# A spectral filter and gated unit: the filter's second copy made by VectorE and ScalarE, earlier x loads, a new timetable

## The chip, the cores and the metric

The kernel runs on one core of a Trainium2 chip. The core has a matrix engine (TensorE, PE in the profile), two vector engines (VectorE, DVE, and ScalarE, ACT), GpSimd (POOL) and SyncE (SP); the last two issue most of the DMAs here. The metric is device time in microseconds (us) of the whole kernel, the median over runs.

## What is computed

Each of 8 batches of x (3200 x 256) is filtered in the frequency domain along its 3200 rows, then goes through a gated linear unit with a causal convolution of 5 taps:

```python
X = np.fft.rfft(x, axis=1)
y = np.fft.irfft(X * (filt_r + 1j * filt_i)[None], n=3200, axis=1)
for k in range(5):
    gate_pre += conv_w[k] * yp[:, k:k + S, :]     # yp: y with 4 rows of zeros ahead
gate = 1.0 / (1.0 + np.exp(-gate_pre))
out = (gate * (y @ w_val)) @ w_out
```

## The kernel before

The transform over 3200 = 100 x 32 rows is done by matrix products, batch by batch. A batch passes these stages, whose short names are those of the tasks in the code:

- lx: GpSimd issues 8 DMAs that bring x as bf16 tiles xt (`load_x`, L201). s1: products with the first table (L468). so: eviction from PSUM to the tile so. t: VectorE transposes it in blocks into tt (L487).
- s2: products with the second table w_t (L497), in 7 groups u of two frequency slices (the last of one). xs: eviction. z: VectorE multiplies xs with the filter f_t (L513). ia: products with the inverse tables a_t and b_t (L528). ue: eviction into the tile u.
- The way back: batch 0 (the only one in TURN) is turned by VectorE, tasks k, from u into vt (`back`, L569). All other batches write u to a DRAM scratch (wr, L551) and read it back in another order (lv, L561), both issued by SP.
- ib: last inverse products (L579). ye: ScalarE evicts into yt (L588). ha: a small memset on GpSimd.
- For 7 blocks c of 512 rows: cv, the convolution on PE (L618, for batches 6 and 7 L632); ga, the sigmoid (L642); vl, the product with w_val (L652); gv, VectorE's product of both (L667); op, the product with w_out (L675); oe, eviction; st, the store issued by SP (L690).

Evictions so, xs, ue and oe may go to either vector engine; one helper, `copy`, does them (L459 on ScalarE, L461 on VectorE).

The filter tile f_t is 128 partitions x 2 (real, imaginary, index w) x 2 x 13 slices x 256, in bf16. GpSimd loads it in two cuts (FCUT: slices 0 to 5 and 6 to 12), each with w = 0 and 1, into partitions 0 to 31 (t = 0) and 64 to 95 (t = 1), three DMAs each, 24 in all (L261, L264, L267). Partitions 32 to 63 and 96 to 127 hold the same values once more. In `sp_setup` SP issues eight DMAs for that, from f_t to f_t (L294), each waiting for its three loads.

Behind the filter, `gate_loads` (task hold) lets GpSimd copy one value out of the last part of f_t (L449). Tasks lx of batch 1 on, and the loads of w_val and w_out (task wts, `load_w`), come behind it on GpSimd. pd is a memset of the unused part of batch 0's u (L544). cid, cia and cim build the last inverse table ci_t; here cid depends on the last transpose of batch 0.

The order of all instructions is fixed when the program is built. Class `Plan` holds tasks with an engine (or two) and a cost for each, dependencies, tiles taken and given back, and a rank. Its `run` plays them through in assumed time: whenever an engine is free, the ready task of least rank goes there. `stay` is added to the rank when PE would change between kinds of work, `lean` when a task that could go to ScalarE would go to VectorE. Each engine then executes its own instructions strictly in the order that came out; costs only shape that order. Transfers not in the plan (x of batch 0, the filter) are given by assumed landing times. The rank is a formula: for each stage a number from LAG (and FIRST for batch 0), 8 for each batch, and a STEP for each task of the stage.

Of the kernel before, what the change touches and what calls it, by code (L numbers as in the profile page):

```python
# [9 lines left out]
BF16 = mybir.dt.bfloat16  # L10
# [9 lines left out]
NM = 13  # L20
NV = 4 * NS
TURN = (0,)

LAG = dict(lx=-461, s1=-523, so=-124, t=307.5, pd=-178, s2=25, xs=106.5, z=302, ia=221,
           ue=176.5, k=-315, ib=312, ye=-498, cv=280, ga=-531.5, vl=-166.5, gv=-478, op=322.5,
           oe=-241.5)
FIRST = dict(lx=-94, s1=139, so=28.5, t=553.5, pd=153, s2=134, xs=-578.5, z=-363, ia=13, ue=-57,
             k=231.5, ib=193.5, ye=245.5, cv=72, ga=-202.5, vl=160, gv=-113, op=346.5, oe=277)
CONV = 1.2
SMALL = (6, 7)  # L30
STEP = dict(lx=0.95, s1=2.5, so=2.05, t=1.9, pd=0.75, s2=1.9, xs=0.25, z=1.15, ia=0.85, ue=2.25,
            k=0.1, ib=0.9, ye=1.65, cv=2.5, ga=2.2, vl=1.2, gv=0.95, op=1.35, oe=0.55)
STAY, LEAN = 32, 139
# [9 lines left out]
class Plan:  # L43
# [5 lines left out]
    def __init__(self, room, slots, stay=1.0, lean=0.0):  # L49
        self.tasks, self.room, self.stay = {}, dict(room), stay  # L50
        self.lean, self.slots = lean, list(range(slots))

    def add(self, name, engines, rank, deps, emit, take=(), give=(), land=0.0, mode=None,
            ps=0, free=()):
# [86 lines left out]
def kernel(  # L141
# [142 lines left out]
    def sp_setup():  # L284
# [162 lines left out]
    def gate_loads():  # L447
        hold = g1.tile([128, 1], BF16, name="hold")
        nc.gpsimd.tensor_copy(hold[...], f_t[:, 1, 1, NM - 1, 0:1])  # L449
# [245 lines left out]
    plan = Plan(dict(xt=NXT, so=1, t=1, xs=3, z=3, u=1, e=2, v=1, y=2, g=NGB, gv=NGB, o=NOB), 4,  # L695
# [6 lines left out]
    def dma(name, us, rank, dep, give=(), land=2.3, mode=0):  # L702
        add(name, {"DQ": us}, rank, dep, None, land=land, mode=mode)
        add(name + "+", {"none": 0.0}, rank, [name], None, give=give)

    for b in range(B):
        turned = b in TURN
        t0 = NCH * b

        def at(stage, n=0, b=b, t0=t0):  # L710
            return t0 + LAG[stage] + (FIRST.get(stage, 0) if b == 0 else 0) + STEP.get(stage, 1) * n

        for j in range(NCH):
            if b:
                add(f"lx{b},{j}", {"POOL": 0.6}, at("lx", j), ["hold"],
                    lambda e, b=b, j=j: load_x(b, j), take=("xt",), land=1.5)
                add(f"dx{b},{j}", {"DQ": 1.22}, at("lx", j), [f"lx{b},{j}"], None, land=2.0, mode=1)
            dep = [f"dx{b},{j}"] if b else [f"x0{j}", "cfa"]
            dep = dep + ([f"s1{b},{j - 1}"] if j else [])
            add(f"s1{b},{j}", {"PE": 0.45}, at("s1", j), dep, lambda e, b=b, j=j: s1(b, j),  # L720
                ps=1, take=("so",) if j == 0 else (), give=("xt",), mode=0)
            add(f"so{b},{j}", two(0.93, 1.14), at("so", j), [f"s1{b},{j}"],
                lambda e, b=b, j=j: so(b, j, e), free=[(f"s1{b},{j}", 0)])
        for q in range(4):
            add(f"t{b},{q}", {"DVE": 1.17}, at("t"), [f"so{b},{j}" for j in range(NCH)]
# [3 lines left out]
        add(f"pd{b}", {"POOL": 1.2} if turned else {"none": 0.0}, at("pd"),  # L729
            ["pool"] + ([f"pd{b - 1}"] if b else []),  # L730
            lambda e, b=b: pad(b), take=("u",) if turned else ("u", "e"))
        for u, (m0, nm) in enumerate(UCH):
            half = 0 if m0 + nm <= FCUT[0][1] else 1
            add(f"s2{b},{u}", {"PE": 0.11 * nm}, at("s2", u), ["wa"]
# [3 lines left out]
            add(f"xs{b},{u}", two(0.13 + 0.4 * nm, 0.04 + 0.55 * nm), at("xs", u),  # L738
                [f"s2{b},{u}"], lambda e, b=b, u=u: xs(b, u, e), free=[(f"s2{b},{u}", 0)])
            add(f"z{b},{u}", {"DVE": 0.06 + 0.55 * nm}, at("z", u), [f"xs{b},{u}", f"fl{half}"],  # L740
                lambda e, b=b, u=u: zed(b, u), give=("xs",))
            add(f"ia{b},{u}", {"PE": 0.22 * nm}, at("ia", u),
                [f"z{b},{u}", f"te{u // 2},1", f"pd{b}"],
                lambda e, b=b, u=u: inva(b, u), ps=1, give=("z",), mode=1)
            add(f"ue{b},{u}", two(0.13 + 0.4 * nm, 0.04 + 0.55 * nm), at("ue", u),
                [f"ia{b},{u}"], lambda e, b=b, u=u: ue(b, u, e), free=[(f"ia{b},{u}", 0)])
            if not turned:
                add(f"wr{b},{u}", {"SP": 0.45}, at("ue", u), [f"ue{b},{u}"],
                    lambda e, b=b, u=u: wr(b, u), land=1.0)
                dma(f"wq{b},{u}", 0.44 * nm, at("ue", u), [f"wr{b},{u}"])  # L750
        if turned:
            for q in range(4):
                add(f"k{b},{q}", {"DVE": 1.87}, at("k"), [f"ue{b},{u}" for u in range(len(UCH))]
# [3 lines left out]
        else:  # L757
            add(f"wd{b}", {"none": 0.0}, at("ue"), [f"wq{b},{u}+" for u in range(len(UCH))],
                None, take=("v",), give=("u",))
            for j in range(NCH):  # L760
                add(f"lv{b},{j}", {"SP": 0.8}, at("ib", j) - 2, [f"wd{b}"],
                    lambda e, b=b, j=j: lv(b, j), land=1.0)
                dma(f"lq{b},{j}", 0.68, at("ib", j), [f"lv{b},{j}"])
        for j in range(NCH):
            add(f"ib{b},{j}", {"PE": 0.37}, at("ib", j),
# [4 lines left out]
            add(f"ye{b},{j}", {"ACT": 0.79}, at("ye", j), [f"ib{b},{j}"],  # L770
                lambda e, b=b, j=j: ye(b, j), free=[(f"ib{b},{j}", 0)])
        add(f"ha{b}", {"POOL": 0.2}, at("ib"), [f"ye{b},0"], lambda e, b=b: halo(b))
        for c in range(NB):
# [3 lines left out]
            if c == p:  # L777
                add(f"cv{b},{c}", {"PE": CONV if tiny else 1.08 * f}, at("cv", c),
# [4 lines left out]
            add(f"ga{b},{c}", {"ACT": 0.77 * f + 0.16}, at("ga", c), [f"cv{b},{p}"],  # L783
# [82 lines left out]
```

## Time and profile before

| | us |
|---|---|
| median of 3 runs | 303.32 (301.4 to 303.38) |
| profiled execution | 303.88 |
| its span | 302.1 |
| PE busy | 261.7 (87%) |
| VectorE busy | 255.6 (85%) |
| ScalarE busy | 252.6 (84%) |
| GpSimd busy | 59.4 (20%) |

The mean granted TensorE clock is 0.969. In 40 equal slices of the span (7.55 us each), with the busy share in tenths:

```profile
PE   2831679889998799999989999999999999999992
DVE  7788788989999879999999999999998975466471
ACT  3964779999899788998899989999998978877863
PEclk9999956999999799999999999999999999999998
DMA  6999499999799979799998998748644994885656
```

A row reads from left to right in time; 9 is 90% or more. PEclk is the clock granted to PE in tenths of full speed. The engines work side by side, so a share of busy time doesn't tell by itself what sets the end.

### The profile page before, as it was taken

The page shows a single profiled execution, that of the slowest core. Times are in us where ns is not written, and L with a number is a line of the kernel's source. Part 1 is how long each engine was busy: PE and PEld are TensorE (multiplying, and loading weights), DVE is VectorE, ACT ScalarE, POOL GpSimd, SP SyncE. Part 2 cuts the span into 40 slices and gives each one's busy share as a digit, 9 for nine tenths or more (in the row PEclk, how much of TensorE's full clock was granted, in tenths as well). Part 3 has the DMA queues.
Part 4 walks back from the last instruction along what each step waited for, and adds up shares of the span by engine and source line. Part 5 has one row for each costly group of instructions (what it writes and reads, how often), then busy time and mean ns, then how long its engine had stood idle before and what let it go on. Part 6 is the DMA issues. An engine that isn't in the chain of part 4 may idle for free.

```text
span 302.1 us, 9397 instructions
## 1 busy us (share of the span) xinstructions
PE 261.7 (87%) x3924; PEld 158.1 (52%) x3924; DVE 255.6 (85%) x284; ACT 252.6 (84%) x301; POOL 59.4 (20%) x123
## 2 busy tenths in 40 slices
PE   2831679889998799999989999999999999999992
PEld 0121426345556435673567456745667667767661
DVE  7788788989999879999999999999998975466471
ACT  3964779999899788998899989999998978877863
POOL 8665457630140041004100400000000000000000
PEclk9999956999999799999999999999999999999998
DMA  6999499999799979799998998748644994885656
GB/s 91 189 163 166 89 175 134 151 189 237 197 252 261 369 187 225 216 330 294 236 278 283 241 249 248 248 177 257 215 160 183 315 326 156 297 289 203 242 203 239
DMA packets 53514, 67.70 MB, mean 224 GB/s; under 512 B 7840, under 2 KB 34336, under 8 KB 53472
## 3 DMA queue, kind: packets, MB, share of 16 engines
q1 hardware_dynamic: 41264, 51.79, 51.5%
q0 software_dynamic: 12208, 15.31, 31.8%
q8 instruction: 31, 0.51, 0.7%
q14 instruction: 11, 0.09, 0.1%
HBM read 42.54 MB, written 38.14 MB: 267 GB/s over the span
## 4 chain that ended last, share of the span: by engine, by line
PE 46%; ACT 18%; DVE 13%; DMA 12%; issue 5%; POOL 4%; ACTq 0%; DVEq 0%; POOLq 0%; SPq 0%
PE ps L675 12%; PE ps L652 10%; PE ps L618 10%; DMA xt<-in_x_dram 5%; ACT yt L588 5%; PE ps L579 4%; DVE gv L667 4%; DVE xs L461 4%; PE ps L528 3%; ACT gt L642 3%; DVE z L513 3%; ACT u L459 3%; PE ps L632 3%; POOL xt L201 2%; DMA f_t<-in_filt_r_dram 2%
## 5 line engine op out<-in xcount | busy, mean ns | idle before, releaser
L667 DVE TENSOR_TENSOR gv<-ps,gt 128x1024 bf16<-128x1024 f32 (+1 forms) x56 | 61.4, 1103 | 19.3 <-PE ps L652 14.7
L513 DVE TENSOR_TENSOR z<-xs,f_t 128x2048 bf16<-128x2048 bf16 (+1 forms) x56 | 62.3, 1140 | 1.9 <-DMA f_t<-f_t 1.4
L642 ACT ACTIVATE gt<-ps 128x1024 bf16<-128x1024 f32 (+1 forms) x56 | 50.9, 939 | 9.2 <-PE ps L618 5.5
L459 ACT ACTIVATE so<-ps 128x1024 bf16<-128x1024 f32 x51 | 49.7, 1031 | 8.2 <-PE ps L468 7.1
L588 ACT ACTIVATE yt<-ps 128x800 bf16<-128x800 f32 x64 | 51.2, 854 | 4.8 <-PE ps L579 4.7
L201 POOL DMA_DIRECT2D xt<-in_x_dram x64 | 35.4, 557 | 96.7 <-PE ps L468 66.2
L468 PE MATMUL ps<-xt,cf_t 100*128 100x512 bf16 x128 | 45.2, 443 | 9.8 <-DMA xt<-in_x_dram 6.7
L652 PE MATMUL ps<-yt,wv_t 128*128 128x512 bf16 (+1 forms) x224 | 52.5, 356 | 0.6 <-ACT xs L459 0.3
L675 PE MATMUL ps<-wo_t,gv 128*128 128x256 bf16 x400 | 51.2, 273 | 1.3 <-ACT yt L588 0.5
L618 PE MATMUL ps<-yt,dg_t 64*64 64x512 bf16 (+1 forms) x880 | 49.3, 357 | 1.3 <-ACT yt L588 1.1
L459 ACT ACTIVATE u<-ps 128x1024 bf16<-128x1024 f32 (+1 forms) x42 | 40.9, 989 | 9.7 <-PE ps L528 9.5
L459 ACT ACTIVATE o<-ps 128x1024 f32<-128x1024 f32 (+1 forms) x41 | 38.0, 938 | 7.1 <-PE ps L675 5.7
L675 PEld LDWEIGHTS <-gv 128*128 128x128 bf16 x400 | 37.2, 98 | 10.6 <-issue 2.9
L487 DVE STREAM_TRANSPOSE tt<-so 128x1024 f32<-128x1024 f32 x32 | 38.3, 1223 | 2.1 <-ACT so L459 2.1
L528 PE MATMUL ps<-z,a_t 64*64 64x256 bf16 x416 | 28.0, 288 | 11.5 <-DVE z L513 8.8
L579 PE MATMUL ps<-ci_t,vt 104*128 104x100 f16 (+1 forms) x512 | 33.5, 212 | 1.7 <-ACT u L459 0.6
L618 PEld LDWEIGHTS <-dg_t 64*64 64x64 bf16 x880 | 24.5, 108 | 18.0 <-issue 5.1
L579 PEld LDWEIGHTS <-vt 104*128 104x128 bf16 (+1 forms) x512 | 28.7, 100 | 10.0 <-issue 5.1
L461 DVE CAST xs<-ps 128x1024 bf16<-128x1024 f32 (+1 forms) x30 | 33.2, 1127 | 0.0
L497 PE MATMUL ps<-tt,w_t 64*64 64x256 bf16 x416 | 23.0, 292 | 8.2 <-DVE tt L487 5.6
L652 PEld LDWEIGHTS <-wv_t 128*128 128x128 bf16 x224 | 19.3, 97 | 17.7 <-issue 3.4
L459 ACT ACTIVATE xs<-ps 128x1024 bf16<-128x1024 f32 (+1 forms) x26 | 24.8, 994 | 3.5 <-PE ps L497 3.3
(98 smaller groups left out, 202.2 us busy)
## 6 DMA issues: line engine op xcount, KB each, us to landing
out_dram<-o SPq DMA_DIRECT2D x48, 512.0 KB
xt<-in_x_dram POOLq DMA_DIRECT2D x64, 200.0 KB, 8.5
escr<-u SPq DMA_DIRECT2D x42, 256.0 KB
vt<-escr SPq DMA_DIRECT2D x56, 192.0 KB
out_dram<-o SPq DMA_DIRECT2D x8, 128.0 KB
f_t<-f_t SPq DMA_DIRECT2D x4, 224.0 KB
escr<-u SPq DMA_DIRECT2D x7, 128.0 KB
vt<-escr SPq DMA_DIRECT2D x56, 16.0 KB
```

Of the source, the lines that this page charges most:

```text
L201: nc.gpsimd.dma_start(out=xt[0:L], in_=src)
L459: nc.scalar.activation(dst, src, AF.Copy, **kw)
L461: nc.vector.tensor_copy(dst, src)
L468: nc.tensor.matmul(ps[:, 512 * h:512 * h + 512], lhsT=cf_t[0:L].rearrange("p h c i -> p (h c i)"), rhs=xv[:, DQ // 2 * h:DQ // 2 * h + DQ ...
L513: nc.vector.tensor_tensor(z[:, :, :, 0:nm * D], st.pop(("XS", b, u))[:, :, 0:nm * D].unsqueeze(1) .to_broadcast((128, 2, 2, nm * D)), f_t[ ...
L579: nc.tensor.matmul(ps[:, o:o + L], lhsT=v[rows, RC * j + a, 128 * dh:128 * dh + 128], rhs=ci_t[rows, way, :], start=True, stop=True)
L588: nc.scalar.activation(y[:, :, H:H + N].rearrange("p h (a r) -> p h a r", r=R)[:, :, :, RC * j:RC * j + RC], ps[:, :].rearrange("p (h n) - ...
L618: nc.tensor.matmul(ps[o:o + 64, 512 * dh:512 * dh + w], lhsT=dg_t[rows, dh, k, :], rhs=y[rows, dh, BLK * c + k:BLK * c + k + w], start=(k ...
L642: nc.scalar.activation(g[:, :, 0:w], two_banks(ps, w), AF.Sigmoid)
L652: nc.tensor.matmul(ps[:, 512 * eh:512 * eh + w], lhsT=wv_t[:, dh, eh, o:o + 128], rhs=y[:, dh, H + BLK * c:H + BLK * c + w], start=(dh == ...
L667: nc.vector.tensor_tensor(o, i0, i1, op=ALU.mult)
L675: nc.tensor.matmul(ps[:, D * a:D * a + D], lhsT=gv_[:, eh, 128 * a:128 * a + 128], rhs=wo_t[:, c % 2 * pair(b, c), eh, :], start=(eh == 0) ...
```

## The change

- `sp_setup` no longer copies f_t; a new function `twin` does it as eight tasks fd (cut h, w, t), each on VectorE or ScalarE as the planner decides. Every task z of a cut waits for the four fd of that cut.
- `gate_loads` and the task hold are gone. Batch 1's loads and the weights wait only for "pool", a time at which GpSimd is assumed to be done with the filter (22 us, 20 before); each lx waits for the one before it. cid depends on wd (the second table's phases) and no longer on batch 0's transposes.
- The rank formula is replaced by a list TIMES of 1,159 numbers, taken in the order of the `add` calls and divided by 100; STAY and LEAN go from 32 and 139 to 2.6 and 5.1. Assumed landing times of the filter change too.

```diff
-LAG = dict(lx=-461, s1=-523, so=-124, t=307.5, pd=-178, s2=25, xs=106.5, z=302, ia=221,
...
-STAY, LEAN = 32, 139
+STAY, LEAN = 2.6, 5.1
+
+TIMES = [6045, -2430, 3242, -301, 64, -3062, 3825, -4640, -1646, -3299, -5370, 2181, -2530, 351,
...
+        queue = engines.keys() - {"none", "DQ"}
+        rank = next(self.times) / 100 if queue else 0.0
...
-        for m0, m1 in FCUT:
-            for w in range(2):
-                for t in range(2):
-                    p = 64 * t
-                    nc.sync.dma_start(out=f_t[p + 32:p + 64, w, :, m0:m1, :],
-                                      in_=f_t[p:p + 32, w, :, m0:m1, :])
...
-    def gate_loads():
-        hold = g1.tile([128, 1], BF16, name="hold")
-        nc.gpsimd.tensor_copy(hold[...], f_t[:, 1, 1, NM - 1, 0:1])
+    def twin(half, w, t, e):
+        m0, m1 = FCUT[half]
+        p = 64 * t
+        copy(e, f_t[p + 32:p + 64, w, :, m0:m1, :], f_t[p:p + 32, w, :, m0:m1, :])
...
-                add(f"lx{b},{j}", {"POOL": 0.6}, at("lx", j), ["hold"],
+                add(f"lx{b},{j}", {"POOL": 0.6}, ["pool"] + ([f"lx{b},{j - 1}"] if j else [f"lx{b - 1},{NCH - 1}"] if b > 1 else []),
...
-            add(f"z{b},{u}", {"DVE": 0.06 + 0.55 * nm}, at("z", u), [f"xs{b},{u}", f"fl{half}"],
+            add(f"z{b},{u}", {"DVE": 0.06 + 0.55 * nm}, [f"xs{b},{u}"] + [f"fd{half},{w},{t}" for w in range(2) for t in range(2)],
...
-    add("pool", {"none": 0.0}, -100, [], None, land=20.0)
-    add("wts", {"POOL": 5.0}, 8.5, ["hold"], lambda e: load_w())
+    add("pool", {"none": 0.0}, [], None, land=22.0)
+    add("wts", {"POOL": 5.0}, ["pool"], lambda e: load_w())
...
-    add("dq", {"DQ": 30.0}, -100, [], None, mode=0)
-    for n, when in (("fl0", 27.0), ("fl1", 31.0)):
+    add("dq", {"DQ": 23.5}, [], None, mode=0)
+    for n, when in (("fr0,0", 16.5), ("fr0,1", 19.6), ("fr1,0", 22.8), ("fr1,1", 25.8)):
         add(n, {"none": 0.0}, [], None, land=when)
+    for h, (m0, m1) in enumerate(FCUT):
+        for w in range(2):
+            for t in range(2):
+                fm = m1 - m0
+                add(f"fd{h},{w},{t}", two(0.2 + 0.5 * fm, 0.06 + 0.14 * fm), [f"fr{h},{w}"],
+                    lambda e, h=h, w=w, t=t: twin(h, w, t, e))
...
-    add("cid", {"DVE": 4.5}, 13, ["t0,3"], lambda e: ci_dve())
+    add("cid", {"DVE": 4.5}, ["wd"], lambda e: ci_dve())
...
-    add("hold", {"POOL": 0.2}, 0, ["fl1", "pd0"], lambda e: gate_loads())
```

More of the change, by code (lines that the diff above doesn't have):

```diff
@@ L43, with __init__, add @@
 class Plan:
-    def __init__(self, room, slots, stay=1.0, lean=0.0):
+    def __init__(self, room, slots, times, stay=1.0, lean=0.0):
         self.tasks, self.room, self.stay = {}, dict(room), stay
-        self.lean, self.slots = lean, list(range(slots))
-    def add(self, name, engines, rank, deps, emit, take=(), give=(), land=0.0, mode=None,
+        self.lean, self.slots, self.times = lean, list(range(slots)), iter(times)
+    def add(self, name, engines, deps, emit, take=(), give=(), land=0.0, mode=None,
             ps=0, free=()):
+        queue = engines.keys() - {"none", "DQ"}
+        rank = next(self.times) / 100 if queue else 0.0
         self.tasks[name] = dict(engines=engines, rank=rank, deps=deps, emit=emit, take=take,
@@ L728 @@
                 give=("so",) if q == 3 else ())
-        add(f"pd{b}", {"POOL": 1.2} if turned else {"none": 0.0}, at("pd"),
+        add(f"pd{b}", {"POOL": 1.2} if turned else {"none": 0.0},
             ["pool"] + ([f"pd{b - 1}"] if b else []),
@@ L811 @@
+    add("pc", {"none": 0.0}, [], None, land=1.5)
+    add("cfd", {"DVE": 2.0}, ["pc"], lambda e: cf_dve())
+    add("cfa", {"ACT": 0.35}, ["cfd"], lambda e: cf_act())
+    add("wd", {"DVE": 7.5}, ["cfd"], lambda e: w_dve())
+    add("wa", {"ACT": 1.65}, ["wd"], lambda e: w_act())
+    add("ey", {"DVE": 0.9}, ["wd"], lambda e: eye())
     for i in range(len(TCH)):
-        add(f"tp{i}", {"PE": 1.2}, 0.5 + 4 * i, ["wa", "ey"], lambda e, i=i: tab_pe(i),
+        add(f"tp{i}", {"PE": 1.2}, ["wa", "ey"], lambda e, i=i: tab_pe(i),
@@ L821 @@
+    add("cia", {"ACT": 0.35}, ["cid"], lambda e: ci_act())
+    add("cim", {"DVE": 0.3}, ["cia"], lambda e: ci_mul())
     for h in range(2):
[L822 to L823 removed]
+        add(f"dg{h}", {"ACT": 1.1}, ["ey"], lambda e, h=h: diag(h))
     plan.room["xt"] -= NCH
```

82 lines of the change are left out of this document (32 added, 50 removed), and 89 rows, old and new, of the table TIMES.

## The prediction

> **What bounds the kernel now.** I began with busy time by stage, in ten windows of 30 us. Columns: window, its length, then busy time (with the number of instructions) of PE, PE's weight loads, VectorE, ScalarE and GpSimd, the granted TensorE clock, the share of the 16 DMA engines, GB/s.
>
> ```profile
> 0.00:30.00 30.00, 11.88 (x104) 4.22 (x108) 23.93 (x72) 17.23 (x29) 21.09 (x47) 1.00 1.01 153
> 30.00:60.00 30.00, 23.93 (x264) 12.26 (x257) 25.88 (x22) 25.86 (x29) 18.24 (x34) 0.77 0.86 137
> 60.00:90.00 30.00, 28.10 (x393) 15.48 (x395) 27.57 (x27) 28.33 (x33) 7.31 (x14) 1.00 0.95 218
> ...
> 210.00:240.00 30.00, 29.20 (x522) 20.25 (x518) 28.60 (x29) 27.93 (x34) 0.21 (x2) 1.00 0.63 214
> ```
>
> From 60 us on PE is busy 28 to 29 us in 30 and the two vector engines nearly as much: over 60 to 270 us PE idles 10.3 us in all (210 less 199.73). In the first 60 us it idles 24.2. There the DMA engines are full (share 1.01). Next I read the chain of waits for the first 60 us: start, length, what.
>
> ```profile
> 18.20 7.26 DMA f_t<-in_filt_r_dram
> 25.74 5.53 DMA f_t<-in_filt_i_dram
> 31.40 2.78 DMA f_t<-f_t
> 34.34 0.19 POOL hold L449
> 34.83 0.89 POOL xt L201 x2
> 38.68 8.87 DMA xt<-in_x_dram
> 47.59 1.05 PE ps L468 x2
> ```
>
> So the start waits for the filter, then for its last copy inside SBUF, then for a GpSimd instruction that holds back batch 1's x, then for that x. The timeline of VectorE (start, length, instruction, and idle time before it with what ended it) shows what this does to batch 0:
>
> ```profile
> 28.20 3.50 DVE L513 TENSOR_TENSOR z<-xs,f_t 128x2048 bf16<-128x2048 bf16 x3 [0.43 <-DMA f_t<-in_filt_i_dram]
> 34.50 2.36 DVE L513 TENSOR_TENSOR z<-xs,f_t 128x2048 bf16<-128x2048 bf16 x2 [1.39 <-DMA f_t<-f_t]
> 41.09 7.42 DVE L569 STREAM_TRANSPOSE vt<-u 128x1024 f32<-128x1024 f32 x4
> 49.72 4.62 DVE L487 STREAM_TRANSPOSE tt<-so 128x1024 f32<-128x1024 f32 x4 [1.21 <-ACT so L459]
> ```
>
> The products of the filter's first half start at 28.20, those of the second at 34.50, 0.3 after the last copy landed; the turn back of batch 0 (vt) at 41.09 ends at 48.51, and only then can batch 0 go on to its inverse, gate and outputs. The start of vt is the number that I move. Last, the DMA queues between 5 and 35 us:
>
> ```profile
> q0 software_dynamic: 3177, 3.12, 72.4%
> q1 hardware_dynamic: 640, 1.70, 27.9%
> ```
>
> q1 is there the eight copies and nothing else of size: 27.9% of 30 us of sixteen engines is 8.4 us for 1.66 MB, or 5.0 us a MB.
>
> **What leaves.** Eight copies (four of 192 KB, four of 224) leave SP's queue and the DMA engines. In the timeline SP issued them at 15.24, 16.76, 17.95, 22.47, 23.78, 26.39, 28.91 and 31.40, each as its piece of filter had landed. Seven of them (1.44 MB, 7.2 us of the engines) ran in front of the last filter piece, three (0.58 MB, 2.9 us) in front of the first half's last. By DMA alone these land at 31.4 - 7.2 = 24.2 and 22.5 - 2.9 = 19.6. Issue puts a floor under the first: GpSimd issues 24 filter loads of 0.53 us from 8.04 and waited 2.3 for x loads to drain, so it ends near 23.1, and the fastest filter landing took 3.1. I take 26.5. The copy's own 2.78 goes too. The hold (0.19, behind a wait of 6.69) leaves GpSimd; queued behind it were batch 1's x loads and the weights.
>
> **What is added.** Eight copies across 32 partitions, 3,072 or 3,584 bf16 each, on VectorE or ScalarE as the planner chooses. The trace has no such instruction on VectorE. Nearest by kind is L349, SBUF to SBUF with one source: 128x1664 f32, 6,656 bytes a partition, in 1.11 us, so 1.02 and 1.19 by bytes. Slow side: z's 2,048 bf16 in 1.22 (two sources), so 1.8 and 2.1. Fast side: the planner's own 0.90 and 1.04. I take 1.1. On ScalarE, 1,024 elements take 1.02 and 512 take 0.59, so 2.7 and 3.2; I take 2.95. Neither can gain by itself, since nothing there is dropped for them.
>
> **Where they lie.** From 17.0 to 41.09 VectorE is busy 6.56 + 4.93 + 4.43 + 3.88 = 19.8 of 24.1 us (finer windows; the last less 0.91 of vt), ScalarE 4.13 + 1.76 + 4.79 + 3.07 = 13.8. The inverse table's build (4.6 + 1.0 on VectorE, 21.71 to 27.77) no longer waits for batch 0's transposes; VectorE idles some 2.8 us between 10 and 17, so that much moves ahead. With three copies on ScalarE (8.9 us into its idle 10.3) and five on VectorE, VectorE needs 19.8 + 5.5 - 2.8 = 22.5: vt starts 1.6 earlier if VectorE stays the limit. If instead the filter is the limit, the second half's products start at 26.5 plus one copy (1.1 to 3.2), near 28.7 in place of 34.50: 5.8 earlier. In the first case ScalarE can still take casts (VectorE did 2.6 us of u and xs there). I take the middle, **3.7 us**. All eight on VectorE: 19.8 + 8.8 - 2.8 = 25.8, vt 1.7 later; that is the dear end.
>
> A copy waits for its filter piece, and VectorE runs in order, so transposes and products queue behind it. The planner's landings (16.5, 19.6, 22.8, 25.8) and mine (19.6 and 26.5 for the halves' ends) differ by 0.7 at most: that is the stall, inside the middle taken.
>
> **The x loads.** Pairing the list of ranks with the order of the add calls, GpSimd's ranks are 15.92 and 20.46 for batch 1's first two loads, 38.05 for the weights, 44.04 for the pad memset, 44.29 for the third load. So two loads go right behind the filter and six behind ten weight loads (6.1 us of issuing) and the pad (1.4). From 26.5, 0.48 MB of weights and 1.64 MB of x at q0's rate (3.12 MB in 72.4% of 30 us, 0.144 MB a us) take 14.7 us: x is complete near 41 in place of 47.6. Cover: vt then still runs, so this is worth only the 1.21 us that the transposes at 49.72 waited for the last so. If the six come no sooner, that 1.2 is gone.
>
> **A port rule.** One pair of rows speaks of contention. GpSimd made iotas of 128x128 in 0.24 and 0.26 us, but:
>
> ```profile
> 6.87 1.11 DVE L349 TENSOR_SCALAR vt<-vt 128x1664 f32<-128x1664 f32 x1
> 7.06 1.04 POOL L208 IOTA af<- 128x100 f32 x1
> ```
>
> the smaller one, begun inside L349, ended at 8.10, 0.12 after it. So a VectorE copy may hold GpSimd for its length, and GpSimd issues the filter and x loads. Four copies of 1.1 before the last filter issue would hold it 4.4 us at most; filter loads land 3.8 to 6.8 us after issue, so the DMA engines have that much queued, and I count nothing in the sum. Without that cover it is 4.4. The Trainium skill, page "SBUF — State Buffer", section "SBUF: two separate sides", states the same: a VectorE instruction in a two-port mode and a GpSimd one exclude each other for the whole instruction, descriptor writing for GpSimd's DMAs included. The trace agrees for an iota; no row of before shows it for a DMA issue.
>
> **The timetable.** Every rank is new. Over 60 to 270 us it can take away at most 10.3 us of PE idle time, and it can add some. No row says which: I take 0, between -5 and +10.
>
> **The sum.** 3.7 + 1.2 = 4.9 us. The profiled execution took 303.88 (span 302.1, 1.78 around it): 299.0. The median of runs lies 0.56 below it, so **298.4 us**, own range 296 to 301.
>
> **Rivals.**
> 1. *VectorE gets all the copies.* vt is 1.7 later instead of 3.7 earlier: 298.4 + 3.7 + 1.7 = 303.8. For: VectorE idles only 4.3 us before vt and is three times as fast at a copy. Against: ScalarE's 10.3 idle.
> 2. *VectorE's copies hold GpSimd.* The filter's issues come 4.4 later and so does all behind: 298.4 + 4.4 = 302.8. For: the iota. Against: the 3.8 to 6.8 us of transfers queued. It decides once the holds before the last filter issue pass some 4 us.
> 3. *Slower: the new order stalls the full stage.* Engines run in order by costs that differ from the trace (so on ScalarE 0.93 planned, 1.02 run; s1 0.45 planned, 0.94 run at 40.07 us, where the granted clock is 0.50). One late operation then holds all behind it; VectorE's gate products already wait 14.7 us for PE, in 17 waits. If the idle of PE over 60 to 270 doubles, +10.3: 308.7. It turns slower once that idle passes 10.3 + 4.9 + 3 = 18 us. Against: the present order meets the same mismatch with 4.9% idle.
> 4. *More than the start.* The new order halves that idle: -5.1, 293.3. For: PE has 24.2 us idle in the first 60 us, and work of batch 1 that comes sooner can fill it.
> 5. *The loads aren't where they are said to be*, behind the weights: only the 1.2 falls, 299.6; kept inside the forecast.
>
> **Chances.** Forecast 0.45 (0.33 of it faster by over 1%, 0.12 within), rival 1 0.08 and rival 2 0.07 (both within), rival 3 0.20 (0.19 slower, 0.01 within), rival 4 0.20 (faster). The 1% that a measurement of this kernel can tell puts the bounds at 300.3 and 306.4. Faster 0.53, same 0.28, slower 0.19. Range 292 to 306: it holds the forecast, rivals 1 and 2 and most of rival 4, and leaves out most of rival 3.
>
> **What would show it.** Right: no f_t<-f_t transfers; the second half's first product at 28 to 31; vt starting 36 to 39.5; two x loads by 27 and x complete near 41; eight copies of 0.9 to 1.2 on VectorE or 2.7 to 3.2 on ScalarE; PE idle of 8 to 13 over 56 to 266. Wrong: vt at 41 or later (rival 1), GpSimd's DMA issues stretched beyond 0.57 under VectorE's copies (rival 2), or PE idle over 18 in the full stage (rival 3).

## The result, and the profile after

| | before | changed |
|---|---|---|
| median of 17 runs each, us | 303.01 (300.89 to 306.35) | 304.83 (303.57 to 306.52) |
| ratio, 95% interval | | 1.0083 [1.0056, 1.0109] |
| profiled execution, span, us | 303.88, 302.1 | 303.57, 301.8 |
| batch 0's turn (vt) starts | 41.09 | 46.90 |
| batch 1's transposes start (t1 from here on) | 49.72 | 54.02 |
| from there to the end of the span | 252.4 | 247.8 |
| PE idle between t1 and 31 us before the end | 11.8 of 221.4 | 8.4 of 216.8 |

The changed kernel is 0.8% slower. The ratio compares fast runs alone: two of the 17 of before, at 305.69 and 306.35, count as slow and are left out of it. The profiled execution of the changed kernel is the fastest of its 17 runs, 1.26 us below their median, and that of before lies 0.87 above its own. So the spans hide the loss, and the ratio decides. The rows for t1 and for what follows it say what happened in these two executions: the start became 4.3 us longer and the rest 4.6 shorter. Of the 4.6, 2.1 us come from where the two executions lie about their medians; about 2.5 are left as the gain of the rest, an estimate.

Busy time by stage after the change (window, length, then busy time and instructions of PE, its weight loads, VectorE, ScalarE and GpSimd, the granted clock, the DMA share, GB/s):

```profile
0.00:30.00 30.00, 12.35 (x86) 3.65 (x86) 25.74 (x75) 22.57 (x30) 26.89 (x53) 1.00 0.90 125
30.00:60.00 30.00, 18.41 (x229) 11.59 (x229) 24.64 (x21) 20.34 (x24) 14.33 (x26) 0.89 0.79 128
60.00:90.00 30.00, 26.61 (x384) 13.65 (x375) 28.60 (x26) 27.10 (x31) 5.97 (x11) 1.00 0.77 170
...
210.00:240.00 30.00, 30.00 (x498) 19.52 (x488) 29.35 (x29) 28.65 (x34) 0.21 (x2) 1.00 0.57 191
```

PE did 18.41 us of work between 30 and 60 where it had done 23.93. Later it makes up for it: 30.00 of 30 in the window where it had 29.20. The DMA engines are no longer full in the first 30 us (0.90 after 1.01), and GpSimd is busy there for 26.89 after 21.09. The queues between 5 and 35 us show why the DMA share fell: q1, which had carried the copies at 27.9%, is no longer among them.

```profile
q0 software_dynamic: 5021, 3.82, 92.3%
```

The chain of waits through the same stretch (start, length, what):

```profile
22.28 1.17 POOL f_t L346
...
24.50 1.33 POOL xt L286
...
33.63 3.67 DMA xt<-in_x_dram
37.35 1.03 PE ps L548 x2
```

Between the two x loads stand the ten weight loads. So only one of batch 1's eight x loads came much sooner: the second was issued at 33.63 and the other six from 35.50 on, where before the change all eight had gone out from 34.83 on. The hold is gone as planned, but now GpSimd's own stream of issues is the chain, and its end is again an x load of batch 1. VectorE's timeline (start, length, instruction, number, and the idle time ahead with what ended it) shows what became of batch 0:

```profile
16.67 0.95 DVE L541 COPY f_t<-f_t 32x3072 bf16<-32x3072 bf16 x1
...
24.62 1.08 DVE L541 COPY f_t<-f_t 32x3584 bf16<-32x3584 bf16 x1
...
29.73 1.08 DVE L541 COPY f_t<-f_t 32x3584 bf16<-32x3584 bf16 x1
30.84 2.36 DVE L593 TENSOR_TENSOR z<-xs,f_t 128x2048 bf16<-128x2048 bf16 x2
...
41.41 1.23 DVE L593 TENSOR_TENSOR z<-xs,f_t 128x2048 bf16<-128x2048 bf16 x1 [3.16 <-ACT xs L539]
...
46.90 7.22 DVE L649 STREAM_TRANSPOSE vt<-u 128x1024 f32<-128x1024 f32 x4 [0.44 <-ACT u L539]
54.02 4.58 DVE L567 STREAM_TRANSPOSE tt<-so 128x1024 f32<-128x1024 f32 x4
```

Six copies (three of each size) stand on VectorE, two (2.76 and 3.19 us) on ScalarE. All six lie ahead of the first product, those of the second half too, which the first half's products don't need. The four transposes of batch 0 stand between them and end at 27.32 (before: 21.78). So the first product starts at 30.84 where it had started at 28.20, although GpSimd had issued the last piece of the filter earlier (23.97, before 25.74). The first product of the second half starts at 35.90 (before: 34.50). Then PE, with batch 1's s1 between batch 0's products, waits 2.45 us until 37.35 for that second x load, and VectorE idles 3.16 ahead of 41.41. Two casts of batch 1's so (1.22 and 1.23 us) also stand on VectorE ahead of vt.

One group of the full stage reads the other way, VectorE's gate products (busy time, mean ns | idle time ahead of them, and what ended most of it):

```profile
L747 DVE TENSOR_TENSOR gv<-ps,gt 128x1024 bf16<-128x1024 f32 (+1 forms) x56 | 60.8, 1103 | 13.5 <-PE ps L732 10.1
```

Before, the same 56 instructions waited 19.3 us in all, 14.7 of them for PE.

### The profile page after: what moved, and what is told of

Same layout as the page of the kernel before. It is cut to its first block, busy times and chain, and to the rows that moved or that the text cites. A ratio compares the mean times of both kernels' runs of the same rounds, so it can differ in the third digit from the quotient of the medians.

```text
span 301.8 us, 9355 instructions
## 1 busy us (share of the span) xinstructions
PE 258.3 (86%) x3924; PEld 156.8 (52%) x3924; DVE 263.6 (87%) x294; ACT 256.2 (85%) x299; POOL 63.0 (21%) x122
## 4 chain that ended last, share of the span: by engine, by line
PE 48%; DMA 14%; DVE 14%; POOL 9%; ACT 8%; issue 6%; SPq 0%; DVEq 0%; POOLq 0%; ACTq 0%
PE ps L755 11%; PE ps L698 11%; PE ps L732 11%; DMA vt<-escr 8%; PE ps L659 5%; PE ps L608 4%; DVE gv L747 3%; DVE so L541 3%; PE ps L712 3%; DMA out_dram<-o 3%; DMA f_t<-in_filt_r_dram 2%; PE ps L548 2%; POOL xt L286 2%; ACT so L539 2%; DVE vt L649 2%
## 5 line engine op out<-in xcount | busy, mean ns | idle before, releaser
L747 DVE TENSOR_TENSOR gv<-ps,gt 128x1024 bf16<-128x1024 f32 (+1 forms) x56 | 60.8, 1103 | 13.5 <-PE ps L732 10.1
L722 ACT ACTIVATE gt<-ps 128x1024 bf16<-128x1024 f32 (+1 forms) x56 | 52.1, 945 | 10.4 <-PE ps L712 5.8
L286 POOL DMA_DIRECT2D xt<-in_x_dram x64 | 36.4, 570 | 108.6 <-PE ps L548 89.3
L668 ACT ACTIVATE yt<-ps 128x800 bf16<-128x800 f32 x64 | 52.1, 846 | 7.0 <-PE ps L659 6.5
L548 PE MATMUL ps<-xt,cf_t 100*128 100x512 bf16 x128 | 43.5, 424 | 11.6 <-DMA xt<-in_x_dram 9.3
L539 ACT ACTIVATE so<-ps 128x1024 bf16<-128x1024 f32 x42 | 42.2, 1042 | 6.6 <-PE ps L548 4.2
L539 ACT ACTIVATE u<-ps 128x1024 bf16<-128x1024 f32 (+1 forms) x41 | 40.0, 982 | 4.7 <-PE ps L608 4.3
L539 ACT ACTIVATE o<-ps 128x1024 f32<-128x1024 f32 (+1 forms) x37 | 36.8, 999 | 6.2 <-PE ps L755 5.3
L539 ACT ACTIVATE xs<-ps 128x1024 bf16<-128x1024 f32 (+1 forms) x36 | 35.3, 998 | 3.6 <-PE ps L577 3.3
L608 PE MATMUL ps<-z,b_t 64*64 64x256 bf16 x416 | 28.1, 283 | 0.0
```

Source lines behind the costliest of these rows:

```text
L286: nc.gpsimd.dma_start(out=xt[0:L], in_=src)
L539: nc.scalar.activation(dst, src, AF.Copy, **kw)
L548: nc.tensor.matmul(ps[:, 512 * h:512 * h + 512], lhsT=cf_t[0:L].rearrange("p h c i -> p (h c i)"), rhs=xv[:, DQ // 2 * h:DQ // 2 * h + DQ ...
L608: nc.tensor.matmul(ps[64 * h:64 * h + 64, 512 * t + D * a:512 * t + D * a + D], lhsT=tab[rows, h, m0 + a, :], rhs=z[rows, w, h, D * a:D * ...
L668: nc.scalar.activation(y[:, :, H:H + N].rearrange("p h (a r) -> p h a r", r=R)[:, :, :, RC * j:RC * j + RC], ps[:, :].rearrange("p (h n) - ...
L722: nc.scalar.activation(g[:, :, 0:w], two_banks(ps, w), AF.Sigmoid)
```

## The experiments

Two theories stood at the outset. A: the new order is better in the full stage and worse in the start, and what the start costs hides the gain. B: the copies on VectorE are what costs, by their time or by holding GpSimd. Later came C: the hold had been of use, because it kept batch 1's x from sharing the DMA engines with the filter.

The edits below act on the order once the planner has made it: `move` takes tasks out and puts them right behind another one, `put` adds tasks on an engine, `to` gives tasks to an engine; PSUM slots are then dealt out anew. "New order" is the changed kernel's, "old" that of before.

| | order of the start | filter's second copy by | hold | rest | ratio to before [95%] | vt | t1 | span less t1 |
|---|---|---|---|---|---|---|---|---|
| before | old | DMA | yes | old | 1 | 41.09 | 49.72 | 252.4 |
| changed | new | engines | no | new | 1.0083 [1.0056, 1.0109] | 46.90 | 54.02 | 247.8 |
| e1 | new | DMA | no | new | 1.0114 [1.0067, 1.0162] | 48.39 | 55.52 | 248.2 |
| e2 | new, weights late | engines | no | new | 1.0102 [1.005, 1.0154] | 45.99 | 53.11 | 252.0 |
| e3 | new, transposes first | engines | no | new | 1.0141 [1.0101, 1.0182] | 47.08 | 54.20 | 250.6 |
| e4 | old, first placing | engines | no | old | 1.0175 [1.0121, 1.023] | 45.12 | 52.65 | 253.5 |
| e5 | old, cut too soon | DMA | yes | new | 1.0104 [1.0045, 1.0164] | 47.85 | 54.99 | 250.9 |
| e6 | old, cut too soon | DMA | no | new | 1.0189 [1.0125, 1.0253] | 50.67 | 57.78 | 250.4 |
| e7 | old | DMA | no | old | 1.0176 [1.01, 1.0253] | 44.49 | 52.02 | 252.4 |
| e8 | new | engines, two sources | no | new | 304.81 us, one run | 47.90 | 55.02 | 248.0 |
| e9 | old | DMA | yes | new | 0.9881 [0.982, 0.9943] | 39.48 | 48.40 | 249.1 |
| e10 | old, second placing | engines | no | old | 1.0066 [1.0039, 1.0093] | 41.24 | 50.65 | 254.2 |
| e11 | as e10 | engines | no | new | 0.9988 [0.995, 1.0025] | 41.37 | 50.77 | 249.2 |
| e12 | as e10, nearly | engines | yes | new | 0.9966 [0.9935, 0.9998] | 41.64 | 50.16 | 249.0 |
| e13 | new, mended | engines | no | new | 1.006 [1.0027, 1.0092] | 43.81 | 51.53 | 252.8 |
| e14 | e12, memset late | engines | yes | new | 0.9914 [0.9883, 0.9945] | 39.85 | 47.38 | 249.1 |
| e15 | as e9 | DMA | yes | new | 0.9955 [0.9928, 0.9981] | 40.89 | 50.06 | 248.5 |

The last three columns come from one profiled execution each. The pair e9 and e15, one kernel on two chips, differs by 1.66 us at t1: single profiles are read no closer than that, and the ratios carry the verdicts.

### e1: new order, copies by transfers again

```diff
+        for m0, m1 in FCUT:      # in sp_setup, as before
+            ... nc.sync.dma_start(out=f_t[p + 32:p + 64, ...], in_=f_t[p:p + 32, ...])
-        copy(e, f_t[p + 32:p + 64, w, :, m0:m1, :], f_t[p:p + 32, w, :, m0:m1, :])
```

> The changed kernel with its new order untouched, but the second copy of the filter is made again by eight transfers from SP, and the eight copy tasks of VectorE and ScalarE put out nothing. Theory A (the new order is what holds batch 0's start: transposes split up, x loads behind the weights): the turn back vt still starts at 43 or later (46.9 in the changed kernel, 41.1 before), because TensorE still waits near 37 for x that lies behind the weights; total 303 to 305 us. Rival B (the copies' own cost: 6.2 us of VectorE, 5.9 of ScalarE and GpSimd held while they run): vt back at 41 or earlier, total 299 to 301. Either way GpSimd's DMA issues of over 0.6 us should go.

306.59 us. vt came at 48.39, no better than with the copies, though none of them stands on an engine. The first product started at 27.67 and the next one only at 34.59, behind an idle 5.70 us that ended with ScalarE's xs. PE's row shows why xs was late (PE first, then VectorE):

```profile
31.87 1.03 PE L553 MATMUL ps<-xt,cf_t 100*128 100x512 bf16 x2 [6.74 <-DMA xt<-in_x_dram]
34.59 1.23 DVE L598 TENSOR_TENSOR z<-xs,f_t 128x2048 bf16<-128x2048 bf16 x1 [5.70 <-ACT xs L544]
```

PE stood 6.74 us for batch 1's first x load, because the new order puts that load's product ahead of batch 0's next ones. So theory B can't carry the loss: the new order is late by itself.

### e2 and e3: two single moves in the new start

```diff
+    move(["wts"], "lx1,7")                              # e2
+    move([f"t0,{q}" for q in range(4)], "fd0,0,0")      # e3
```

> The changed kernel with one move on GpSimd: the ten weight loads come behind batch 1's eight x loads. Theory A: TensorE's wait for x at 37.35 (2.45 us) goes and vt starts 2 to 3 us earlier, near 44; if the start passes to the end, total 302 to 303. Rival B: vt stays at 46 to 47 and the total at 304.8. Third view (C: the start doesn't matter, the full stage behind takes it up): vt earlier, total within 0.5 of 304.8.

> The changed kernel with one move on VectorE: the four transposes of batch 0 follow each other, and the copies and the small multiply that lay between them come behind. Same work. Theory A: the transposes end near 23.5 (27.3 now) and vt starts 2 to 4 us earlier, unless TensorE, which has a product of batch 1's x among these products, waits for that x at 29; then near 45.5. Rival B: vt unchanged at 46 to 47, since VectorE's work is the same. Total 301.5 to 303.5 by A, 304.8 by B.

Neither helped: 306.49 and 307.22 us. With the weights behind batch 1's x, the 2.45 us wait of PE is gone but vt moves by only 0.91 (45.99): the first product now starts at 32.87, behind the copies. With the transposes together, the first product still starts at 30.85, since the second half's copies on VectorE still lie ahead of it. Breaking one link shows the next one. In their single profiles both also have a rest 3 to 4 us longer than the changed kernel's (252.0, 250.6); why is open.

### e4 and e7: old order, with copies, and without the hold alone

```diff
+    put(["fd0,1,0"], "ACT", "te2,0")                                # e4
+    put(["fd0,0,0", "fd0,0,1", "fd0,1,1"], "DVE", "t0,3")
+    put(["fd1,0,0"], "ACT", "xs0,0")
+    put(["fd1,0,1", "fd1,1,0", "fd1,1,1"], "DVE", "z0,2")
...
+    order[:] = [t for t in order if t[0] != "hold"]                 # e4 and e7
```

> The kernel before with its own order, and of the change only the parts other than the timetable: two copies on ScalarE and six on VectorE, behind the transposes and behind the first three products; the hold gone, so x of batch 1 right behind the filter; the last inverse table built early, with the casts it displaces on ScalarE. Theory A: vt starts at 37 to 39 (41.1 before) and, if the start passes to the end, 299 to 301 us in place of 303. Rival B: vt at 41 or later, 303 to 305. View C: vt earlier, total within 0.7 of 303.

> The kernel before with one thing taken away: the hold. Old order, eight transfers from SP. The part of the change that brings x forward, by itself. If x of batch 1 held the start (my 1.2 us): vt unchanged near 41, 1 us faster, 301 to 302. If the x loads take the DMA engines from the filter: vt 1 to 3 us later and 303 to 305.

e4: 308.12 us. The old order doesn't help the copies when they are put in badly: a copy of the second half, 3.19 us on ScalarE at 26.57, delayed the evictions xs, and VectorE's products stood 3.04 us behind them. e7 is the cleaner run, one instruction less than before, and it took 309.38 us: the hold alone is worth 1.76% in the old kernel, with an interval from 1.0 to 2.53%. Its chain of waits:

```profile
25.66 4.88 DMA f_t<-in_filt_i_dram
...
30.68 6.57 DMA f_t<-f_t
...
37.56 1.24 DVE z L513
```

The last copy inside SBUF was issued at 30.68, 0.7 earlier than before, but took 6.57 us and not 2.78: GpSimd had issued eight x loads between 27.50 and 31.9, and these were on the DMA engines at the same time. So the second half's products start at 37.56 and not at 34.50, and vt at 44.49. That is theory C: without the hold, x goes first and the filter pays. The profiled execution took 306.2 us, the fastest of four (306.2 to 310.21). Its profile shows 2.3 us at t1 and nothing behind it, so less than half of the 5.3 us; where the other three executions lost more isn't shown.

### e5 and e6: old start, new rest, cut at the wrong place

```diff
+    start = ...      # the order of before up to k0,0, batch 0's turn
+    order[:] = lead + start + [t for t in order if t[0] not in done]
```

> Every engine's order is that of the kernel before up to batch 0's turn back vt, with the eight transfers from SP and the hold; behind it the order of the changed kernel. No copies on VectorE or ScalarE. Theory A2 (the new order spends some 6 us in the start and saves some 6 us behind it: from the start of vt to the end 255 us in the changed kernel and 255 with its transfers, 261 before): vt at 41, span 296, time 297 to 299, faster than both. Rival C2 (the rest is only shorter because a late start leaves it a fuller stock of work, or the saving lies in a few lucky places): vt at 41, span 300 to 303, time 302 to 305.

> As the run before it, without the hold: x of batch 1 goes right behind the filter loads, in among the eight transfers. Theory A2: batch 1's x lands 5 us sooner and the filter's transfers 1 to 2 us later; vt at 41 to 43, time 297 to 300. Rival C2: 302 to 305.

306.57 and 309.42 us, both misses, and what both share is the cut: behind it the new order places two of batch 1's evictions (so1,2 and so1,4) on VectorE ahead of vt, and these had to wait for PE's products of batch 1 (1.97 and 1.94 us in e5). With the hold, the second half's products ran nearly as before (35.12), yet vt started at 47.85; without it they came at 39.94, later still than in e7. The pair still speaks for the hold: the ratios are 1.8% without and 1.0% with it, and though their intervals overlap, the four times of each, taken on one chip, don't (308.7 to 310.08 against 305.64 to 307.68).

### e8: VectorE's copies with two sources

```diff
+            V.tensor_tensor(f_t[p + 32:p + 64, w, :, m0:m1, :], src, src, op=ALU.max)
```

> The changed kernel with VectorE's six copies made as the maximum of a tile with itself, so with two sources, 1.8 to 2.1 us each in place of 0.95 to 1.08. If VectorE's one-source copies hold GpSimd: GpSimd's DMA issues of 0.9 to 1.3 us under them go back to 0.51 to 0.57. If it is something else (the queue, the DMA engines), they stay long. The time should be 3 to 6 us above the changed kernel's, since VectorE is busy without a gap there; equal if GpSimd's holds were the dearer part.

The rows of GpSimd in the changed kernel, and then in e8:

```profile
16.64 1.08 POOL L346 DMA_DIRECT2D f_t<-in_filt_r_dram  x1
20.32 0.90 POOL L346 DMA_DIRECT2D f_t<-in_filt_i_dram  x1
22.26 1.19 POOL L346 DMA_DIRECT2D f_t<-in_filt_i_dram  x1
```

```profile
16.43 0.51 POOL L346 DMA_DIRECT2D f_t<-in_filt_r_dram  x1
22.40 0.53 POOL L352 DMA_DIRECT2D f_t<-in_filt_i_dram  x1
```

Under a one-source copy of VectorE an issue takes 0.90 to 1.19 us in place of 0.51 to 0.57. The three such issues of the filter take 1.6 us more in all, and the last of the filter starts at 23.97. With two sources the copies are slower (1.75 us for 3,072 elements, 2.02 for 3,584, where the one-source copies took 0.95 and 1.08), but every filter issue is short again, and the last starts at 22.40. The total of the one run is 304.81 us, the changed kernel's median being 304.83; before took 304.13 on that chip, so one run can't tell a small gain from none. The hold on GpSimd is real. Whether it costs nothing here, or what the slower copies cost, is open. The start tells something else: the first product came at 35.21, 4.37 us later than in the changed kernel, and vt only 1.00 later (47.90). So in the new order the first product alone doesn't set vt; batch 1's s1 on PE is the other link. The Trainium skill, page "SBUF — State Buffer", section "SBUF: two separate sides", has the rule: a VectorE instruction in a two-port mode takes the port that it shares with GpSimd for its whole length, and GpSimd's DMA descriptors wait; two inputs from SBUF bar only a GpSimd instruction that reads SBUF. Both kernels' rows agree with it.

### e9 and e15: old start through the turn, new rest

```diff
+    start = ...      # the order of before up to t1,0, SP's transfers and the hold kept
+    order[:] = lead + start + [t for t in order if t[0] not in done]
```

> Old order, eight transfers and the hold up to and including batch 0's turn back, its last inverse and ScalarE's evictions of it; from batch 1's transposes on the order of the changed kernel. (The earlier splice was cut too soon: behind the cut, the new order had two casts of batch 1 ahead of vt on VectorE, and vt came at 47.85.) Theory A2 (behind the start the new order is 4 to 5 us the shorter): vt at 41, batch 1's transposes at 49.7, 298 to 300. Rival C2 (the new rest is no shorter; it only had a later start): 302 to 304.

> e9 unchanged, on the same chip as e14, for the comparison: eight transfers, hold, old start, new order behind. 298.5 to 300.5 us if e9's 0.988 stands; 301 or more if its four runs were lucky.

This is theory A by itself, the new rest with the start of before. 299.62 us (4 runs) and 301.47 (12 runs on another chip): ratios 0.9881 [0.982, 0.9943] and 0.9955 [0.9928, 0.9981]. Both are faster than before, though one kernel's ratio differs by 0.74% of the time between the two chips. The rest took 249.1 and 248.5 us.

### e10 and e11: copies well placed, old rest and new rest

```diff
+    to(["so0,5", "so0,6", "te0,0", "te0,1", "ue0,1"], "ACT")
+    move(["dg0", "dg1"], "ue0,5")
+    move(["cid"], "ey")
+    move(["cia"], "xs0,2")
+    put(["fd0,1,0"], "ACT", "te1,0")
+    put(["fd0,0,0", "fd0,0,1", "fd0,1,1"], "DVE", "t0,3")
+    move(["cim"], "z0,6")
+    put(["fd1,0,0", "fd1,0,1", "fd1,1,0", "fd1,1,1"], "DVE", "z0,2")
+    move([f"lx1,{j}" for j in range(8)], "so0,7")
+    order[:] = [t for t in order if t[0] != "hold"]
...
+    start = ...      # e11: this order up to t1,0, then the new order
```

> The kernel before in its order, the copies on engines, better placed than in e4: three of the first half on VectorE behind the transposes and one on ScalarE, all four of the second half on VectorE behind the first three products; the small tables of ScalarE later; no hold, pad memset behind the x loads. Theory: VectorE needs 4.3 us for the second half's copies in place of waiting to 34.5 for the transfers, so the second half's products start near 33 and vt at 39 to 40.5, and as the start passes on at least one to one in this order (e4, e7), 300.5 to 302.5. Rival (copies and GpSimd hold each other, ScalarE late): vt at 42 or later, 304 to 306.

> The start of e10 up to batch 1's transposes, then the order of the changed kernel. Both theories of e9 and e10 right: vt at 39 to 40.5 and 296 to 299. If only e9's is: 298 to 301. If the new rest is no shorter: as e10.

Each half's copies now stand right ahead of that half's products, and vt starts at 41.24 and 41.37, as before the change. e10 took 305.67 us, e11 303.18, with the same start and on the same chip: the new rest takes away 0.78%.

### e12, e13 and e14: the hold back, the new start mended, the memset late

```diff
+        if n == "lx1,0":                                            # e12, e14
+            redone.append((lambda e: gate_loads(), "POOL", []))
...
+    move([f"t0,{q}" for q in range(4)], "fd0,0,0")                  # e13
+    move(["fd1,0,0", "fd1,1,1", "fd1,1,0", "cim"], "z0,1")
+    move(["fd1,0,1"], "xs0,1")
+    for j in range(8):
+        order[:] = [(n, "ACT") if n == f"so1,{j}" else (n, e) for n, e in order]
+    move([f"{s}1,{j}" for j in range(8) for s in ("dx", "s1", "so")], "ue0,6")
...
-            nc.gpsimd.memset(st["U", b][:, NS:32, :], 0.0)          # e14
+        if n == "lx1,7":
+            redone.append((lambda e: nc.gpsimd.memset(...), "POOL", []))
```

> The start of e11 with two things put back: the hold (so the x loads wait for the last copy, and the pad memset comes ahead of them as before), and ScalarE's ten small table instructions moved into its gap of 4 us ahead of the last evictions of batch 0, where in e10 they held back batch 1's casts by 2.5 us. Copies on engines, new order behind batch 1's first transpose. Theory (GpSimd's x loads and pad memset were what stretched the second half's four copies from 4.3 to 6.0 us, and the tables what made batch 1's transposes wait 2 us): the four copies take 4.3 to 4.5 us, vt at 39 to 40, the transposes of batch 1 at 47.5 to 49, 296.5 to 299 us in all. Rival (they wait for the filter to land): the copies still end near 34 and vt stays at 41; then 299 to 302.

> The changed kernel with its start mended by moves alone: the four transposes together, the second half's copies behind the first half's products, and batch 1's first products and casts behind batch 0's inverse products (their casts on ScalarE). Weights still ahead of six x loads, no hold. Theory A (the order of these places, not the copies, makes the start late; single moves in e2 and e3 only shifted the wait to the next place): first product near 26, vt at 40 to 42, batch 1's transposes at 50 to 51.5 (54.0 in the changed kernel), 301 to 303. Rival (copies and GpSimd set it): vt at 45 or later, 304 to 307.

> e12 with one move: GpSimd's pad memset (1.40 us), which in e12 ran from 23.48 beside VectorE's copies of the first half (4.65 us for three, 2.85 of work), comes behind batch 1's x loads. Theory (a GpSimd memset holds a VectorE copy for its length): the three copies take 2.8 to 3.0, the first product comes at 24.7 to 25, vt at 39.5 to 40.5 and the transposes of batch 1 at 48 to 49.5; 299 to 301 us. Rival (the third copy waited for the filter to land): the copies still end near 26.5, all as in e12, 301 to 302.5.

In e12 and e14 the list of the start also puts ScalarE's small tables earlier; in e12 the memset comes ahead of the x loads again. e13 mended much of the start (vt 43.81, after 46.90; t1 51.53, after 54.02), so both links together do what neither did alone. It didn't mend the total, 305.0 us: its rest took 252.8. Why stays open; the profiled execution, 306.56, is also the slowest of its ten. e12 took 301.93 us. Its rows show a loss that can be mended. VectorE in e12 (first fence; the second line is from a narrower window, which shows the second of the three copies by itself) and GpSimd in the same kernel (second):

```profile
21.90 4.65 DVE L545 COPY f_t<-f_t 32x3072 bf16<-32x3072 bf16 x3
22.88 2.81 DVE L545 COPY f_t<-f_t 32x3072 bf16<-32x3072 bf16 x1
26.64 3.50 DVE L597 TENSOR_TENSOR z<-xs,f_t 128x2048 bf16<-128x2048 bf16 x3
```

```profile
22.96 0.53 POOL L352 DMA_DIRECT2D f_t<-in_filt_i_dram  x1
23.48 1.40 POOL L628 MEMSET u<- 128x1536 bf16 x1
```

Three copies that had taken 2.81 us in e10 took 4.65, with a GpSimd memset of 1.40 beside them. The second copy bears it all: 2.81 us in place of 0.95, from 22.88 to 25.69, with GpSimd's last filter issue and the memset behind it, until 24.88, inside. That is 0.95 us of work begun about when the memset ended. e10 had shown the like at its other four copies: 6.02 us (4.44 in e14), with the memset at 28.51 and x issues among them. So GpSimd can hold VectorE as well. The Trainium skill, page "SBUF — State Buffer", section "SBUF: two separate sides", has this direction too: whichever of the two starts first keeps the pair of ports for its whole instruction, and the other is blocked. The copy of 2.81 us agrees with the blocking. Which of the two came first the trace doesn't tell: the copy is recorded from 22.88, the issue from 22.96. e14 issues the memset behind batch 1's last x load:

```profile
21.95 2.81 DVE L545 COPY f_t<-f_t 32x3072 bf16<-32x3072 bf16 x3
24.86 3.50 DVE L597 TENSOR_TENSOR z<-xs,f_t 128x2048 bf16<-128x2048 bf16 x3
28.38 4.44 DVE L545 COPY f_t<-f_t 32x3584 bf16<-32x3584 bf16 x4
```

The three take 2.81 again, the first product starts 1.78 earlier, and vt at 39.85. e14 took 300.17 us, 0.9914 [0.9883, 0.9945]: faster than both kernels.

## Why the prediction was wrong

The change was forecast to be 4.9 us faster and came out 0.8% slower. That 304.83 us lies inside the wide range of 292 to 306, and near rival 1's 303.8, is luck: neither the forecast's nor that rival's mechanism is what happened, and the late start was partly paid back by a shorter rest. Three kernels between before and the changed kernel form a path of four steps:

| step | from, to | ratio | change | worth in us of 303 |
|---|---|---|---|---|
| the hold goes | before, e7 | 1 to 1.0176 | +1.8% | +5.3 |
| engines copy, well placed | e7, e10 | 1.0176 to 1.0066 | -1.1% | -3.3 |
| new order behind the turn | e10, e11 | 1.0066 to 0.9988 | -0.8% | -2.4 |
| new order of the start | e11, changed | 0.9988 to 1.0083 | +1.0% | +2.9 |

The worths are differences of ratios; with the half widths of both intervals put together (root of the sum of squares) they are uncertain by 0.8, 0.8, 0.5 and 0.5% in turn, and another sequence of the steps could share them out otherwise. Only the first and the third compare runs of one chip and session; across chips one kernel's ratio differed by 0.74% (e9 and e15), so the sizes of the second and the fourth are rough. The second also moves small tables, casts and the pad memset, not the copies alone. That the four add to +2.5 us, the 0.8% of the result, follows from how they are formed and checks nothing.

- **What bounds the kernel, and what leaves.** Right in the main. The start waited for filter, hold and x (the DMA share of 1.01 holds for the first 30 us alone; from 30 to 60 it was 0.86). But the removal of the hold was given no cost of its own, only x that comes sooner. e7 shows the cost: the last copy shares the DMA engines with x. With the copies off them most of it comes back, but the pair is still 0.7% slower than before (e10).
- **"vt 3.7 us earlier".** This step failed. It came 5.81 later. The working weighed VectorE's busy time before vt against the filter's landing and took a middle. Both limits are sums; neither asks in which order the instructions stand. The start's new order put copies that nobody yet needed ahead of the first product, spread the transposes between them, and put batch 1's s1 on PE, and two of its casts on VectorE, between batch 0's products. The second half's first product, expected near 28.7, started at 35.90. Which of these places weighs most isn't settled: copies off the engines (e1), x ahead of the weights (e2) and transposes together (e3) move vt by +1.5, -0.9 and +0.2 us, and only the moves of e13 together by -3.1. e11 keeps copies and rest and takes the old order of the start: vt at 41.37, and 0.95% less time. Even there vt is not earlier than before the change; of the runs with copies on engines only e14 gets it to 39.85, with the hold kept and the memset moved, and that lies between 39.48 and 40.89, the starts in e9 and e15, one kernel. The stall from landings, at most 0.7, was no issue: no copy on VectorE has a wait for a filter piece in its row.
- **Sizes of the copies.** Right: 0.95 to 1.09 on VectorE (1.1 taken), 2.76 and 3.19 on ScalarE (2.95). The split was six and two, not five and three.
- **The x loads.** Misread. One load and not two went ahead of the weights, and six were issued from 35.50 on; with their median landing of 6.4 us x was complete near 45, an estimate, and not near 41. The list of ranks doesn't give the order by itself: in the plan each x load is ready only 1.5 us after the one ahead, and the weights, ready at once, took GpSimd in between. The working held that batch 1's x could cost only the 1.21 us ahead of t1. In the new order it also stood ahead of vt, since PE waited for it (2.45 us) with batch 0's products behind.
- **The 1.21 us at batch 1's transposes.** That wait is gone, as said: the row at 54.02 has none. But vt ends later, so it brought nothing.
- **The port rule at nothing in the sum.** Not refuted, and not settled either, by the one run of e8. The issues were stretched as rival 2 had it, by 1.6 us in all and not 4.4. That the same port lets GpSimd delay VectorE was not in the sum at all: 1.8 us in e12, none of it in the changed kernel, whose memset at 34.17 met no copy.
- **The new timetable at 0, between -5 and +10.** Mis-sized, in the part that it was applied to. With the old order, the rest took 252.4 to 254.2 us in four profiles (mean 253.1); with the new order, 247.8 to 252.8 in thirteen (mean 249.7): about -3.4, or -2.4 by e10 and e11. PE's idle time in that stretch went with it, 11.8, 13.4 and 12.6 us in before, e7 and e10, and 8.4, 10.0 and 10.1 in changed, e9 and e14.
- **Rivals.** 1 (VectorE gets all copies) named the right engine and too few us: six copies, but their places count, not their sum. 2 has its mechanism shown, and no effect on the total can be told from e8's one run. 3 (the new order stalls the full stage) is wrong in its place: the stall is in the start. 4 (more than the start) is right in part for the rest: over 60 to 270 us PE's idle time fell from 10.3 to 7.7 us, about half of what it named. In the first 60 us, where it hoped that batch 1's work would fill PE, the idle time grew from 24.2 to 29.2. 5 came true for the second x load, behind the weights, and cost more than its 1.2, as said above.

Two things stay open. Whether copies on the engines beat transfers once the start is in good order isn't settled. By the ratios e14 (0.9914) lies between e9 and e15 (0.9881 and 0.9955), which are one kernel. Run side by side on one chip, twelve times each, e14's median of 300.17 us lies 1.3 below e15's 301.47, with an uncertainty of some 0.8, an estimate from the spread of the runs; but e14 also has the memset late and other moves. And why e2, e3 and e13 had a rest 3 to 5 us longer than the changed kernel with the same order there. Part of that is which execution was profiled: set against each kernel's median, about 2 us are left, an estimate. The hold in the new start wasn't tried.

## What to carry to other kernels

A new order of the whole program is two changes, one to the start and one to the steady part; splice the old start to the new rest (and cut behind the last instruction that the start must finish) before you call it good or bad. When work moves to an in-order engine, ask what stands behind each instruction there and whether it needs it, not only whether the sum fits. Read an order from what the planner puts out, not from its ranks: a task of lower rank that isn't ready lets another one pass. An instruction that seems only to hold something back may be keeping a shared transfer path free for what is needed first: cost its removal alone.

## What the runs showed of the hardware

A GpSimd memset of 128x1536 bf16 (1.40 us), close behind a DMA issue, lengthened three one-source VectorE copies from 2.81 to 4.65 us (e14, e12). The other way, such a copy stretched one GpSimd DMA issue from 0.51 to as much as 1.19 us; in the three cases it ended 0.10 to 0.11 us after the copy did. By contrast, copies with two sources, 1.75 us long, stretched none of the filter's. In e14's profile the granted clock of PE had no dip in the start (mean 0.996), where the profile of before (0.969) has two slices of the start near half speed. That is no mark of the order: over executions the mean granted clock ranged from 0.966 to 0.996 in e14 and from 0.965 to 0.998 in before on the same chip, and e14's profile is the fastest of its twelve executions and the one with the highest clock. What decides the dip was not tried.
